# Narrowing all float64 weight pieces in two ScalarE operations through a ring tile, with new costs in the hand-written planner

## The chip, the core and the metric

The kernel runs on one core of one Trainium2 chip. The metric is the device time of one execution in microseconds (us). TensorE multiplies matrices, VectorE and ScalarE work element by element, GpSimd does some elementwise work and indirect transfers, and SyncE issues most of the DMA transfers. Each engine works through its own queue of instructions in the order in which the program wrote them.

## The reference

Three stages follow one another.

```python
# attention: q, k, v are (4, 8, 576, 64) float32
scores = scale * np.matmul(q, k.transpose(0, 1, 3, 2))
kth = np.partition(scores, -32, axis=-1)[..., -32:-31]
attn = softmax(np.where(scores >= kth, scores, -1e9))
x = np.matmul(attn, v)                        # as (2304, 512)

# routing: every token goes to one of 8 experts, 288 tokens each, greedily by logit x @ w_gate
h = np.maximum(x[mask] @ w1[e], 0.0)          # w1: (8, 512, 1024)
x[mask] = h @ w2[e]                           # w2: (8, 1024, 512)

# rational layer
h = x @ w_in                                  # w_in: (512, 2048), float64
g = (a0 + a1*h + a2*h*h + a3*h*h*h) / (1 + |b0|*|h| + |b1|*h*h + 1e-6)
out = (g @ w_out).astype(np.float32)          # w_out: (2048, 512), float64
```

[...] The kernel makes float32 values out of the bits of the float64 ones ("narrowing"), and splits each float32 matrix into a high and a low float16 part, scaled by powers of two, so that TensorE can multiply in float16 with three products.

## The kernel before

`w_in` and `w_out` are cut into 32 pieces of 128 rows by 512 values, 16 of each. A piece is fetched into a raw tile of 128 x 1024 words (`fetch`, L329). Pieces 0 to 5 lie in the tile `win`, 6 to 13 in `wout`, 14 to 17 in `nraw0` to `nraw3` at first; later ones take the places that come free, and the last eight (24 to 31) lie in `region`, which held the first expert's weights.

Narrowing a piece takes ScalarE operations on the top 16 bits of each value (`heads`, L364), then VectorE operations (`mantissa`, L402, with `signed` or `apply_sign`). There are two ways before the change. Pieces 6 to 19 (`quick`, L352) take two ScalarE operations, Abs (L370) and Relu with a scale and a bias (L374), both written into one of three ring tiles; VectorE then ors in the sign bit (`signed`, L392) and the mantissa (`mantissa`, L405). The other 18 pieces take three ScalarE operations in place, Sign into a byte (L380), Abs (L381) and Relu (L382); VectorE then ors in the mantissa (L405) and multiplies by the sign (L409). Behind both, ScalarE squares the piece with a sum (L303); when the four pieces of a block are squared, VectorE works out a power of two as scale, ScalarE writes the high part (`high`, L433) and VectorE the low part (`low`, L437). The low part ends the use of the raw tile, and the next fetch goes into its place.

The order of instructions is worked out when the program is built, by a planner, the class `Flow`. A task has an engine, a cost in us, dependencies and a rank. `Flow` keeps a clock for each engine and always emits the task that can start first, and among equals the one of lowest rank. Costs and start times are the planner's own numbers; on the chip every engine takes its queue in the emitted order. `take` (L159) keeps a task from starting before the task that used the same buffer some turns earlier has been emitted: with `ZR = 3` ring tiles, the first head of a piece waits for the last VectorE part of the piece three before.

The program runs through these stages:

- Attention (up to about 476 us), with an order written out by hand.
- The attention tail, `finish_attention`, a `Flow` of its own called `last`: the last units' softmax, transposes of the weights (`st_transpose`, tile `pt`), their evacuation by ScalarE (`st_spill`, tile `pT`), the product with v (`st_av`, tile `po`), and the router's logits. Tasks of rank 1000 and above fill in: the ScalarE heads of pieces 0 to 5, VectorE's parts of pieces 0 to 2 (`EV = 3`), and `conv_stats` of the first expert's weights. `drain` lets such a task in only where no other task of its engine could start within 0.3 of its cost.
- Routing (511 to about 610 us), seven phases of four iterations in `search`. In each iteration VectorE compares, TensorE counts, VectorE makes the next thresholds. In two gaps of an iteration the planner is called to emit ready tasks of the main `Flow`. The VectorE tasks in a gap have to fit its budget, `J1` or `J3` and `J2`; tasks of ScalarE may run up to `LA` ahead. VectorE's parts of pieces 3 to 31 are put there as halves of 256 values (`in_parts`). `tail` emits one TensorE task, mostly a product of the first expert's weight split, whose result ScalarE copies (L1432).
- `flow.early()` emits what is left until no task is left that is not marked `late`: the blocks of `w_in`, the first three blocks of `w_out`, and the first expert. The fourth block of `w_out` (pieces 28 to 31, rank 6) and the second expert are late. Then `flow.rest()` orders everything else: for each of eight experts 16 units of the rational layer (`add_unit`), weight splits of the next expert (`add_weights`), its products (`add_expert`). Output products need the scales of all blocks of `w_out` (`settle_out`).

```python
def in_parts(cost, fn, deps, rank, late, hv=None):
    w = 512 // (hv or HV)                       # HV = 2
    return [
        flow.add("V", 0.06 + (cost - 0.06) * w / 512, lambda o=o: fn(slice(o, o + w)), deps, rank, late)
        for o in range(0, 512, w)
    ]

def allowed(t, s):                              # in Flow.fill(budget, before)
    v = self.free["V"]
    if t.engine == "V":
        return s <= v + 0.05 and v + t.cost <= v0 + budget + 0.01
    return t.engine != "P" and s <= v + before

J1, J2, J3, T1, T2, T3, J4 = (float(c) for c in "0.6 0.37 0.6 1 1 0 0".split())
```

Of the kernel before, what the change touches and what calls it, by code (L numbers as in the profile page):

```python
# [8 lines left out]
F32 = mybir.dt.float32  # L9
# [175 lines left out]
def kernel(  # L185
# [92 lines left out]
    bias8 = wpool.tile([P, 1], F32, name="bias8")  # L278
    nc.vector.memset(bias8, -896.0 * 2.0**23)
# [50 lines left out]
    SIGN = getattr(mybir.dt, "int8")  # L330
# [17 lines left out]
    QS = int(6)  # L348
    QE = int(20)
    ring, ring_of, ring_users = [], {}, []  # L350

    def quick(n):  # L352
        return QS <= n < QE

    def sign(n):
        return raw_t[n][0].bitcast(SIGN).rearrange("p (n w) -> p n w", w=8)[:, :, 0]

# [6 lines left out]
    def heads(n):  # L364
        top = top_of(n)
        if quick(n):
            def size():
                ring.append(ring.pop(0))
                ring_of[n] = ring[-1]
                nc.scalar.activation(upper_of(n).bitcast(BF16), top.bitcast(BF16), AF.Abs)  # L370

            return [
                ("A", 0.52, size),
                ("A", 0.52, lambda: nc.scalar.activation(  # L374
                    upper_of(n), upper_of(n), AF.Relu, scale=2.0**3, bias=bias16
                )),
            ]
        top = top.bitcast(BF16)
        return [
            ("A", 0.52, lambda: nc.scalar.activation(sign(n), top, AF.Sign)),  # L380
            ("A", 0.52, lambda: nc.scalar.activation(top, top, AF.Abs)),  # L381
            ("A", 0.61, lambda: nc.scalar.activation(  # L382
                value(n).bitcast(U32), top.bitcast(U16), AF.Relu, scale=2.0**19, bias=bias8
            )),
        ]
# [16 lines left out]
    def mantissa(n, o=ALL):  # L402
        mid = raw_t[n][0].rearrange("p (n w) -> p n w", w=2)[:, o, 0]
        up = ring_of[n][:, o] if quick(n) else value(n)[:, o]
        nc.vector.scalar_tensor_tensor(value(n)[:, o], mid, 13, up, op0=OP.logical_shift_right, op1=OP.bitwise_or)  # L405

    def apply_sign(n, o=ALL):
        d = value(n).bitcast(F32)[:, o]
        nc.vector.tensor_tensor(d, d, sign(n)[:, o], op=OP.mult)  # L409
# [4 lines left out]
    EV = 3  # L414

    def add_block(i, n0, dst, s, inv, rows, rank, late, after):
# [54 lines left out]
    with ExitStack() as actx:  # L471
# [61 lines left out]
        with ExitStack() as sctx:  # L533
# [519 lines left out]
            def finish_attention():  # L1053
# [53 lines left out]
                def add_weights_of(u, deps):  # L1107
# [3 lines left out]
                    for hh in range(2):  # L1111
# [15 lines left out]
                        a = last.add("A", 0.67, exp_of, [largest_of[u]] if u in largest_of else [], u)  # L1127
# [5 lines left out]
                def add_turned(u, deps):  # L1133
                    t = last.add("P", 1.1, lambda: st_transpose(u), deps, u)
                    a = last.add("A", 1.01, lambda: st_spill(u), [t], u)
# [88 lines left out]
                for u in range(done["av"], NU):  # L1224
                    if u not in tr_of:
                        tr_of[u] = last.add("A", 1.01, lambda u=u: st_spill(u), [], u)
# [31 lines left out]
                for n in range(6):  # L1258
                    t = []
                    for k in range(3):  # L1260
                        t = [last.add("A", 0.55, lambda n=n, k=k: heads(n)[k][2](), t, 1000 + n)]
                    if n < EV:
                        t = [last.add("V", 0.6, lambda n=n: mantissa(n), t, 1000 + n)]
                        t = [last.add("V", 0.6, lambda n=n: apply_sign(n), t, 1000 + n)]
                for w in (1, 2):
                    for c in range(4):
                        f = last.add("A", 1.04, lambda w=w, c=c: conv_stats(w, 0, c), [], 1000 + (SO if w == 1 else 3) + c)
# [148 lines left out]
        def add_first(which):  # L1416
# [17 lines left out]
            for c in range(4):  # L1434
                t = flow.add("A", 0.95, lambda c=c: conv_hi(which, 0, c), [scaled], -88.0)
# [904 lines left out]
```

## Time and profile before

| | |
|---|---|
| median of three runs | 1280.82 us (1274.78, 1280.82, 1280.97) |
| profiled execution | 1273.43 us, span 1271.7 us |
| TensorE busy in the span | 1142.7 us (90%) |
| VectorE busy | 1152.7 us (91%) |
| ScalarE busy | 1113.9 us (88%) |
| GpSimd busy | 430.7 us (34%) |

The span runs from the first to the last instruction. The profile comes from one execution; its times are us from the start of the span. PE is TensorE's matmul, PEld its weight load, DVE is VectorE, ACT is ScalarE, POOL is GpSimd, SP is SyncE. L303 is line 303 of the kernel. Matmuls overlap, so a busy PE is not PE at its peak. Operations that follow one another on an engine overlap at their ends, so that the distance from start to start is less than the duration.

### The profile page before, as it was taken

Reading aid. Unit: us, or ns where it says so; the run is one execution under the profiler, and the core shown is the slowest. Engines: PE = TensorE matmul, PEld = TensorE weight load, DVE = VectorE, ACT = ScalarE, POOL = GpSimd, SP = SyncE. Lnnn points to the kernel's source line nnn. Section 1 sums busy time; section 2 is a strip of 40 time slices with the busy share of each in tenths; the row PEclk is TensorE's granted clock in tenths of the full one; section 3 lists DMA queues with packets and bytes.
Section 4 is the critical chain, followed back from the end, with each engine's and each line's share of the span. In section 5 each row is a group of like instructions: output and inputs, shape, how many; then the busy total and the mean of one; then the engine's idle time right before and its main releaser. Section 6 shows DMA issues by size and latency. Waiting matters only on the chain.

```text
span 1271.7 us, 26707 instructions
## 1 busy us (share of the span) xinstructions
PE 1142.7 (90%) x9159; PEld 924.6 (73%) x9159; DVE 1152.7 (91%) x4567; ACT 1113.9 (88%) x2150; POOL 430.7 (34%) x431
## 2 busy tenths in 40 slices
PE   6899999999999987687566899999999999999995
PEld 4678787888878876555444677888888888888774
DVE  5999999999999986887789989999999999998895
ACT  5999999999999979867799989998989899887684
POOL 4888888887877850000110001010110001001010
PEclk9999999999999989555688999999999999999998
DMA  5204021020200030921311430303122220200000
GB/s 121 49 10 148 10 57 37 22 49 10 49 1 2 2 133 3 328 105 52 102 55 69 148 129 26 133 26 114 52 86 86 77 76 26 80 1 20 1 20 20
DMA packets 81109, 80.59 MB, mean 63 GB/s; under 512 B 59968, under 2 KB 59968, under 8 KB 80960
## 3 DMA queue, kind: packets, MB, share of 16 engines
q1 hardware_dynamic: 77888, 69.27, 17.1%
q0 software_dynamic: 3072, 9.48, 2.6%
q8 instruction: 76, 1.25, 0.4%
q14 instruction: 73, 0.60, 0.2%
HBM read 69.25 MB, written 9.47 MB: 62 GB/s over the span
## 4 chain that ended last, share of the span: by engine, by line
PE 25%; issue 14%; ACT 6%; DVE 4%; POOL 1%; DMA 1%; POOLq 0%; DVEq 0%
PE pa L1891 3%; PE pa L1893 3%; PE pa L1892 3%; PE ph L1891 3%; PE ph L1892 3%; PE ph L1893 3%; PE po L1892 2%; PE po L1893 2%; PE po L1891 2%; ACT junk L303 1%; POOL out_dram L2261 1%; DMA region<-in_moe_w_dram 1%; DVE wout L437 1%; ACT uv L2152 0%; PE pa L2250 0%
## 5 line engine op out<-in xcount | busy, mean ns | idle before, releaser
L730 DVE MAX8 cd<-sv 128x8 f32<-128x82 f32 (+1 forms) x1008 | 182.5, 229 | 16.5 <-ACT sv L684 16.5
L756 POOL TENSOR_TENSOR win<-sv,sg 128x576 f32<-128x576 f32 x142 | 178.9, 1281 | 52.3 <-ACT sg L751 43.4
L811 POOL TENSOR_TENSOR sv<-ex,sg 128x576 f32<-128x576 f32 x136 | 175.5, 1296 | 44.2 <-DVE sg L808 30.8
L1891 PE MATMUL ph<-x,win 128*128 128x288 f16 x512 | 148.5, 290 | 15.8 <-DVE uv L2173 15.7
L839 PEld LDWEIGHTS po<-vm,pT 128*128 128x128 f32 (+1 forms) x1280 | 143.5, 182 | 19.0 <-ACT pT L823 4.0
L839 PE MATMUL po<-vm,pT 128*128 128x65 f32 (+1 forms) x1280 | 150.2, 266 | 4.8 <-ACT pT L823 3.2
L1892 PE MATMUL po<-g,wout 128*128 128x288 f16 x512 | 146.4, 286 | 4.8 <-DVE g L1882 4.7
L1891 PE MATMUL po<-g,wout 128*128 128x288 f16 x512 | 146.4, 286 | 2.5 <-ACT g L1881 2.5
L1892 PE MATMUL ph<-x,win 128*128 128x288 f16 x512 | 148.5, 290 | 0.0
L1893 PE MATMUL ph<-x,win 128*128 128x288 f16 x512 | 148.4, 290 | 0.0
L1893 PE MATMUL po<-g,wout 128*128 128x288 f16 x512 | 146.4, 286 | 0.0
L1868 POOL DMA_INDIRECT xe<-xrows,rows_i x24 | 24.4, 1017 | 313.6 <-PE pa L1903 160.8
L2261 POOL DMA_INDIRECT out_dram<-ob,tok x24 | 27.3, 1137 | 299.8 <-ACT ob L2257 251.2
L751 ACT ACTIVATE sg<-sv,cut_all 128x576 bf16<-128x576 f32 x142 | 109.2, 779 | 1.4 <-DVE cut_all L736 1.0
L817 PE MATMUL pt<-ident,sv 128*128 128x128 f32 x648 | 93.9, 282 | 13.3 <-POOL sv L811 11.2
L757 DVE MAX8 w<-win 128x8 f32<-128x576 f32 x142 | 105.1, 741 | 0.0
L805 ACT ACTIVATE ex<-sv,nb 128x576 f32<-128x576 f32 x136 | 103.9, 771 | 0.0
L817 PEld LDWEIGHTS pt<-ident,sv 128*128 128x128 f32 x648 | 73.6, 143 | 39.4 <-POOL sv L811 26.7
L671 PE MATMUL s<-region 128*128 128x288 f32 (+5 forms) x400 | 91.7, 385 | 3.7 <-ACT sv L684 2.4
L2149 ACT ACTIVATE z<-ph,inv 128x288 f32<-128x288 f32 x128 | 63.9, 499 | 35.5 <-PE ph L1893 32.5
L684 ACT ACTIVATE sv<-s 128x576 f32<-128x576 f32 x144 | 85.2, 645 | 9.8 <-PE s L671 9.5
L671 PE MATMUL s<-kT,region 128*128 128x288 f32 (+5 forms) x400 | 88.8, 375 | 2.1 <-ACT sv L684 2.0
(361 smaller groups left out, 3510.3 us busy)
## 6 DMA issues: line engine op xcount, KB each, us to landing
region<-in_moe_w_dram SPq DMA_DIRECT2D x16, 2048.0 KB, 8.1
xrows<-x SPq DMA_DIRECT2D x1, 4644.0 KB, 22.6
region<-in_q_dram SPq DMA_DIRECT2D x32, 128.0 KB, 2.9
region<-in_k_dram SPq DMA_DIRECT2D x32, 128.0 KB, 2.9
vm<-in_v_dram SPq DMA_DIRECT2D x32, 128.0 KB, 2.9
wout<-in_moe_w_in_dram SPq DMA_DIRECT2D x8, 511.8 KB, 8.0
region<-in_moe_w_out_dram SPq DMA_DIRECT2D x8, 511.8 KB, 3.5
win<-in_moe_w_in_dram SPq DMA_DIRECT2D x6, 511.8 KB, 6.0
```

The source lines that it names most:

```text
L671: nc.tensor.matmul(ps[p0 : p0 + n, g, o : o + w], qT[:, hh, j, p0 : p0 + n], kT[:, bb, c : c + w], start=True, stop=True,)
L730: nc.vector.max(cd[:, g, :], sv[:, o : o + n])
L751: nc.scalar.activation(sg, sv_t[u, hh], AF.Sign, bias=cut_all[:, 2 * u + hh, 7:8], scale=-OVER, accum_out=t["sum"][:, c : c + 1],)
L756: nc.gpsimd.tensor_tensor(win, sv_t[u, hh], sg, op=OP.mult)
L757: later.append(lambda c=c, win=win: nc.vector.max(t["w8"][:, c, :], win))
L805: nc.scalar.activation(ex, sv, AF.Exp, bias=t["nb"][:, c : c + 1], scale=SCALE)
L811: nc.gpsimd.tensor_tensor(sv, ex, sg, op=OP.mult)
L817: nc.tensor.transpose(pt[:, c // 4, c % 4, :], pr[:, c * P : (c + 1) * P], ident)
L839: nc.tensor.matmul(po[p0 : p0 + n, i, hh, :], sb[:, hh * (R + 1) + c, p0 : p0 + n], vm[:, bb, hh, c, :], start=(c == 0), stop=False,)
L1891: nc.tensor.matmul(acc, ah, bh, start=first, stop=False)
L1892: nc.tensor.matmul(acc, ah, bl, start=False, stop=False)
L1893: nc.tensor.matmul(acc, al, bh, start=False, stop=last)
```

## The change

All 32 pieces take the two ScalarE operations in a ring tile, and VectorE's `signed` and `mantissa`; the form with three operations, with `sign` and `apply_sign`, is gone, and so is its constant `bias8`. In the attention tail pieces 0 to 5 are narrowed whole (`EV = 6`): the ring there consists of three parts of the v tiles that are no longer read, which GpSimd sets to zero. Behind the tail the ring list is emptied and filled with the three ring tiles of before. The costs of many planner tasks are replaced by larger numbers. The budgets of the routing gaps, the ranks, the number of ring tiles and the latencies of the planner stay.

```diff
-    QS = int(6)
-    QE = int(20)
     ring, ring_of, ring_users = [], {}, []
...
     def heads(n):
-        top = top_of(n)
-        if quick(n):
-            def size():
-                ring.append(ring.pop(0))
-                ring_of[n] = ring[-1]
-                nc.scalar.activation(upper_of(n).bitcast(BF16), top.bitcast(BF16), AF.Abs)
...
-        top = top.bitcast(BF16)
+
+        def size():
+            ring.append(ring.pop(0))
+            ring_of[n] = ring[-1]
+            nc.scalar.activation(upper_of(n).bitcast(BF16), top_of(n).bitcast(BF16), AF.Abs)
+
         return [
-            ("A", 0.52, lambda: nc.scalar.activation(sign(n), top, AF.Sign)),
-            ("A", 0.52, lambda: nc.scalar.activation(top, top, AF.Abs)),
-            ("A", 0.61, lambda: nc.scalar.activation(
-                value(n).bitcast(U32), top.bitcast(U16), AF.Relu, scale=2.0**19, bias=bias8
-            )),
+            size,
+            lambda: nc.scalar.activation(upper_of(n), upper_of(n), AF.Relu, scale=2.0**3, bias=bias16),
         ]
...
-    EV = 3
+    EV = 6
...
-            if quick(n):
-                first = flow.add("A", 0.52, lambda n=n: heads(n)[0][2](), t, rank + 0.5, late)
-                t = flow.add("A", 0.52, lambda n=n: heads(n)[1][2](), [first], rank + 0.5, late)
-                t = in_parts(0.6, lambda o, n=n: signed(n, o), [t], rank + 0.4, late)
-                t = in_parts(0.6, lambda o, n=n: mantissa(n, o), t, rank + 0.3, late)
+            if n >= EV:
+                first = flow.add("A", 0.77, lambda n=n: heads(n)[0](), t, rank + 0.5, late)
+                t = [flow.add("A", 0.87, lambda n=n: heads(n)[1](), [first], rank + 0.5, late)]
+                t = in_parts(0.81, lambda o, n=n: signed(n, o), t, rank + 0.4, late)
+                t = in_parts(0.77, lambda o, n=n: mantissa(n, o), t, rank + 0.3, late)
                 take(first, ring_users, ZR, t)
-            else:
-                for k in range(3 if n >= 6 else 0):
-                    t = [flow.add("A", (0.52, 0.52, 0.61)[k], lambda n=n, k=k: heads(n)[k][2](), t, rank + 0.5, late)]
-                if n >= EV:
-                    t = in_parts(0.6, lambda o, n=n: mantissa(n, o), t, rank + 0.4, late)
-                    t = in_parts(0.6, lambda o, n=n: apply_sign(n, o), t, rank + 0.3, late)
             norms.append(
-                flow.add("A", 0.61, lambda n=n, g=g: square(value(n).bitcast(F32), sq[:, g : g + 1]), t, rank + 0.2, late)
+                flow.add("A", 0.86, lambda n=n, g=g: square(value(n).bitcast(F32), sq[:, g : g + 1]), t, rank + 0.2, late)
             )
...
-            t = flow.add("A", 0.61, lambda g=g: high(g), [scaled] + (lasts[-1] if lasts else []), rank + LOWS, late)
-            t = flow.add("V", 0.66, lambda g=g: low(g), [t], rank + LOWS + 0.1, late)
+            t = flow.add("A", 0.75, lambda g=g: high(g), [scaled] + (lasts[-1] if lasts else []), rank + LOWS, late)
+            t = flow.add("V", 0.74, lambda g=g: low(g), [t], rank + LOWS + 0.1, late)
...
-                for n in range(6):
-                    t = []
-                    for k in range(3):
-                        t = [last.add("A", 0.55, lambda n=n, k=k: heads(n)[k][2](), t, 1000 + n)]
-                    if n < EV:
-                        t = [last.add("V", 0.6, lambda n=n: mantissa(n), t, 1000 + n)]
-                        t = [last.add("V", 0.6, lambda n=n: apply_sign(n), t, 1000 + n)]
+                for i in (2, 2, 0):
+                    free = v_pad[i][0].rearrange("p b h r d -> p (b h r d)").bitcast(U32)
+                    ring.append(free[:, 512 * len(ring) % 1024 :][:, 0:512])
+                    nc.gpsimd.memset(ring[-1], 0)
+                for n in range(EV):
+                    first = last.add("A", 0.77, lambda n=n: heads(n)[0](), [], 1000 + n)
+                    t = [last.add("A", 0.87, lambda n=n: heads(n)[1](), [first], 1000 + n)]
+                    t = [last.add("V", 0.6, lambda n=n: signed(n, ALL), t, 1000 + n)]
+                    t = [last.add("V", 0.6, lambda n=n: mantissa(n), t, 1000 + n)]
+                    take(first, ring_users, ZR, t)
...
+        ring.clear()
+        ring_users.clear()
         for i in range(ZR):
```

The other costs that change: in the tail `exp_of` from 0.67 to 0.77, `st_spill` from 1.01 to 1.16, `conv_stats` from 1.04 to 1.26. For the first expert's weights `conv_hi` from 0.95 to 1.13 and the copy of a product from 0.27 to 0.38, and the squares of x from 0.52 to 0.82. In `add_weights` `conv_stats` from 1.04 to 1.26, `conv_hi` from 0.95 to 1.16, `conv_lo` from 0.63 to 0.75. In `add_unit` the six ScalarE tasks from 0.43, 0.5, 0.5, 0.46, 0.38, 0.46 to 0.49, 0.59, 0.63, 0.54, 0.44, 0.53, and the seven VectorE tasks from 0.43 to 0.48 to 0.45 to 0.51; its TensorE tasks stay at 1.47.

## Rows read from the trace of the kernel before

**Rows 1.** Stretches: length, busy us (count) of PE, PEld, DVE, ACT, POOL; PEclk, DMA.
```profile
476.00:507.00 31.00, 25.95 (x205) 20.32 (x203) 20.17 (x72) 29.95 (x39) 0.96 (x1) 1.00 0.01 2
...
511.00:596.70 85.70, 71.45 (x793) 49.41 (x794) 74.35 (x360) 64.97 (x124) 6.20 (x14) 0.50 0.49 174
596.70:614.00 17.30, 6.55 (x80) 5.36 (x78) 7.73 (x29) 14.10 (x15) 1.94 (x4) 0.50 0.12 35
614.00:671.20 57.20, 35.35 (x248) 26.53 (x248) 53.36 (x150) 50.50 (x96) 9.21 (x9) 0.80 0.27 87
671.20:690.00 18.80, 11.49 (x65) 7.63 (x65) 18.09 (x64) 17.91 (x39) 0.00 (x0) 0.73 0.31 113
690.00:760.00 70.00, 62.65 (x510) 49.41 (x508) 62.18 (x153) 63.80 (x125) 0.84 (x1) 1.00 0.34 121
760.00:1200.00 440.00, 439.14 (x3619) 354.13 (x3618) 408.99 (x1081) 387.54 (x812) 36.90 (x52) 1.00 0.18 59
1200.00:1272.00 72.00, 55.13 (x432) 42.13 (x430) 55.92 (x141) 49.16 (x107) 6.28 (x11) 0.95 0.06 18
```

**Rows 2.** Timeline of ScalarE in the attention tail: start, length, line, output, input.
```profile
485.96 1.21 ACT L823 ACTIVATE pT<-pt 128x1152 f32<-128x1152 f32 x1
...
491.00 1.41 ACT L380 ACTIVATE win<-win 128x512 int8<-128x512 bf16 x1
492.16 1.21 ACT L823 ACTIVATE pT<-pt 128x1152 f32<-128x1152 f32 x1
```

**Rows 3.** Waits, 470 to 507 us: in total, times, longest.
```profile
PE po L839 <- ACT pT L823: 3.2, 4, 1.3
```

**Rows 4.** Waits in the routing stretch, 511 to 597 us.
```profile
DVE over L1561 <- PE pl L1497: 6.0, 18, 0.6
...
PE pl L1428 <- ACT w2s L1432: 0.9, 1, 0.9
```

**Rows 5.** Line L380, the first of three operations: min/median/max ns, first and last start.
```profile
L380 ACT ACTIVATE region<-region x8: 1322/1329/1388, 561.2 to 607.9; 128x512 int8<-128x512 bf16 x8
L380 ACT ACTIVATE win<-win x6: 1322/1373/1416, 476.8 to 499.8; 128x512 int8<-128x512 bf16 x6
L380 ACT ACTIVATE wout<-wout x4: 1354/1398/1462, 637.6 to 652.7; 128x512 int8<-128x512 bf16 x4
```

**Rows 6.** Line L370, the first of two operations, 611.7 to 700 us.
```profile
L370 ACT ACTIVATE ring<-wout x2: 779/786/792, 634.3 to 635.9; 128x512 bf16<-128x512 bf16 x2
L370 ACT ACTIVATE ring<-nraw x1: 771/771/771, 616.1 to 616.1; 128x512 bf16<-128x512 bf16 x1
```

**Rows 7.** Timeline of ScalarE in routing, two-operation pieces.
```profile
529.72 0.77 ACT L370 ACTIVATE ring<-wout 128x512 bf16<-128x512 bf16 x1
530.35 0.36 ACT L1432 ACTIVATE w1s<-pl 128x256 f16<-128x256 f32 x1
530.60 0.87 ACT L374 ACTIVATE ring<-ring,bias 128x512 uint16<-128x512 uint16 x1
531.32 1.38 ACT L370 ACTIVATE ring<-wout 128x512 bf16<-128x512 bf16 x2
...
532.82 0.65 ACT L303 ACTIVATE junk<-win 128x512 bf16<-128x512 f32 x1
...
533.45 1.58 ACT L374 ACTIVATE ring<-ring,bias 128x512 uint16<-128x512 uint16 x2
```

**Rows 8.** Timeline of ScalarE after routing, a three-operation piece.
```profile
637.56 1.35 ACT L380 ACTIVATE wout<-wout 128x512 int8<-128x512 bf16 x1
638.64 0.51 ACT L1877 ACTIVATE hT<-pe 128x288 f16<-128x288 f32 x1
```

**Rows 9.** Groups of VectorE, 511 to 611.7 us: busy us, mean ns; idle before.
```profile
L392 DVE SCALAR_TENSOR_TENSOR ring<-wout,ring 128x256 uint16<-128x256 uint16 x16 | 7.0, 438 | 0.0
L405 DVE SCALAR_TENSOR_TENSOR wout<-wout,ring 128x256 uint32<-128x256 uint32 x16 | 6.6, 414 | 0.0
...
L409 DVE TENSOR_TENSOR win<-win 128x256 f32<-128x256 f32 x6 | 2.5, 415 | 0.0
```

More of the change, by code (lines that the diff above doesn't have):

```diff
@@ L329 @@
     arrived = [Mark() for _ in range(NP)]
-    SIGN = getattr(mybir.dt, "int8")
     def fetch(slot, n=None):
@@ L1134, in add_turned @@
                     t = last.add("P", 1.1, lambda: st_transpose(u), deps, u)
-                    a = last.add("A", 1.01, lambda: st_spill(u), [t], u)
+                    a = last.add("A", 1.16, lambda: st_spill(u), [t], u)
                     hold(t, "pt", 1, [a])
@@ L1225, in finish_attention @@
                     if u not in tr_of:
-                        tr_of[u] = last.add("A", 1.01, lambda u=u: st_spill(u), [], u)
+                        tr_of[u] = last.add("A", 1.16, lambda u=u: st_spill(u), [], u)
                 for u in range(done["av"], NU):
@@ L1434, in add_first @@
             for c in range(4):
-                t = flow.add("A", 0.95, lambda c=c: conv_hi(which, 0, c), [scaled], -88.0)
+                t = flow.add("A", 1.13, lambda c=c: conv_hi(which, 0, c), [scaled], -88.0)
                 for o in range(c * 1024, (c + 1) * 1024, 256):
                     p = flow.add("P", 0.6, lambda o=o: product(o), [t, copies[0]], -88.0)
-                    copies.append(flow.add("A", 0.27, lambda o=o: copy(o), [p], -90.0))
+                    copies.append(flow.add("A", 0.38, lambda o=o: copy(o), [p], -90.0))
                     take(p, pl_users, 2, [copies[-1]])
@@ L1444 @@
         norms = [
-            flow.add("A", 0.52, lambda t=t: square(x[:, t, 0:DM], xs[:, t : t + 1]), (), XSR) for t in late_tiles
+            flow.add("A", 0.82, lambda t=t: square(x[:, t, 0:DM], xs[:, t : t + 1]), (), XSR) for t in late_tiles
         ]
@@ L2003, in add_weights @@
             got = flow.add("D", 5.8, lambda: load_w(which, e), reading("raw", which, e - 1), rank(0))
-        sums = [flow.add("A", 1.04, lambda c=c: conv_stats(which, e, c), [got], rank(c)) for c in range(4)]
+        sums = [flow.add("A", 1.26, lambda c=c: conv_stats(which, e, c), [got], rank(c)) for c in range(4)]
         steps = scale_steps(which, e)
@@ L2009, in add_weights @@
         for c in range(4):
-            t = flow.add("A", 0.95, lambda c=c: conv_hi(which, e, c), [scaled] + hs[-1:], rank(5 + c))
+            t = flow.add("A", 1.16, lambda c=c: conv_hi(which, e, c), [scaled] + hs[-1:], rank(5 + c))
             if c == 0:
@@ L2014, in add_weights @@
         for c in range(8):
-            all_.append(flow.add("V", 0.63, lambda c=c: conv_lo(which, e, c), [hs[c // 2]], rank(5 + c // 2) + 0.1))
+            all_.append(flow.add("V", 0.75, lambda c=c: conv_lo(which, e, c), [hs[c // 2]], rank(5 + c // 2) + 0.1))
         split_of[which, e] = hs + all_
@@ L2196, in add_unit @@
         p = flow.add("P", 1.47, into, x2_of[e] + last["into"], u)
-        a1 = flow.add("A", 0.43, size, [p, scales[e]], u)
-        a3 = flow.add("A", 0.5, cube, [p, scales[e]], u)
-        v1 = flow.add("A", 0.5, below, [a1], u + 0.05)
-        g1 = flow.add("V", 0.43, below2, [v1], u + 0.05)
-        g2 = flow.add("V", 0.44, cube2, [a1, a3], u + 0.1)
-        v3 = flow.add("V", 0.48, cube3, [g2], u + 0.1)
-        a4 = flow.add("A", 0.46, log, [g1], u + 1.0)
-        a5 = flow.add("A", 0.38, exp, [a4], u + 1.0)
-        v2 = flow.add("V", 0.43, near, [a5], u + 1.2)
-        v4 = flow.add("V", 0.43, nearer, [v2], u + 1.2)
-        v5 = flow.add("V", 0.48, ratio, [v3, v4], u + 1.2)
-        a6 = flow.add("A", 0.46, halves, [v5, bounds[e]], u + 2.0)
-        v6 = flow.add("V", 0.48, lambda: st["steps"][1](), [a6], u + 2.1)
+        a1 = flow.add("A", 0.49, size, [p, scales[e]], u)
+        a3 = flow.add("A", 0.59, cube, [p, scales[e]], u)
+        v1 = flow.add("A", 0.63, below, [a1], u + 0.05)
+        g1 = flow.add("V", 0.45, below2, [v1], u + 0.05)
+        g2 = flow.add("V", 0.45, cube2, [a1, a3], u + 0.1)
+        v3 = flow.add("V", 0.51, cube3, [g2], u + 0.1)
+        a4 = flow.add("A", 0.54, log, [g1], u + 1.0)
+        a5 = flow.add("A", 0.44, exp, [a4], u + 1.0)
+        v2 = flow.add("V", 0.45, near, [a5], u + 1.2)
+        v4 = flow.add("V", 0.45, nearer, [v2], u + 1.2)
+        v5 = flow.add("V", 0.51, ratio, [v3, v4], u + 1.2)
+        a6 = flow.add("A", 0.53, halves, [v5, bounds[e]], u + 2.0)
+        v6 = flow.add("V", 0.51, lambda: st["steps"][1](), [a6], u + 2.1)
         p2 = flow.add("P", 1.47, out_of, [v6] + last["out"] + w_out_done[f // 4], u + OUT)
```

25 lines of the change are left out of this document (6 added, 19 removed).

## The prediction

> **What bounds the kernel now.** I read the stages first [rows 1]: in each row compare the length with the busy time of TensorE, VectorE and ScalarE. From 760 to 1200 us TensorE is busy 439.14 of 440 us, so there it alone sets the pace and nothing that the other engines save counts. The stretches before it are different. From 614 to 671.2 us VectorE is busy 53.36 and ScalarE 50.50 of 57.2 us, TensorE only 35.35; from 671.2 to 690 us both are again over 95% busy, and up to 760 us they stay near 90% while TensorE loses 7.35 us. TensorE's queue after routing is a fixed amount of work, so every microsecond by which ScalarE and VectorE are later in getting the weights narrowed between 614 and 760 us moves the end by about a microsecond. The routing stretch before, 511 to 596.7 us, is a fixed loop of handshakes between VectorE and TensorE; ScalarE is busy 64.97 of 85.7 us there, and 14.10 of the next 17.3 us. What is done there is free; what is left over is paid for after 614 us.
>
> Then I read the narrowing itself. A three-operation piece stands in two places: eight of 18 ran between 561 and 610 us, inside routing and its end, four after it, six in the attention tail [rows 5]. Of the two-operation pieces only three had their heads (the ScalarE operations) after routing [rows 6]. Of the VectorE halves, 16 + 16 + 6 and, in two rows not shown, 6 + 1 ran in the routing gaps: 45 [rows 9]. The code has 116 halves in the flow (pieces 3 to 31, four each), so 71 came after.
>
> **The change, part by part.**
>
> *Price of a head.* What counts on a full engine is the distance from start to start, not the duration. A two-operation piece: 529.72 to 530.35 is 0.63, 530.60 to 531.32 is 0.72, together 1.35 us [rows 7]. A three-operation piece: 637.56 to 638.64 is 1.08 [rows 8]; I take that for the first two operations, which last about the same, and 0.72 for the third: 2.88 us. One piece saves 1.53 us of ScalarE; 18 pieces save 27.5. A square takes 532.82 to 533.45, 0.63 us [rows 7].
>
> The rule of the Trainium skill speaks against so large a saving: its page "ScalarE: Activation LUTs", section "What ACT_TABLE_LOAD costs", has one element per cycle for every function, 186 ns + 0.833 ns for each element with immediate operands, less 93 ns of overlap. That would be 0.52 us for each of the two operations where the row has 1.08, so 1.76 us for a three-operation piece. The trace decides and I use 2.88; by the page the sum below would come out 4 x 1.12 = 4.5 us later.
>
> *Attention tail.* Six pieces lose 1.53 us each: 9.2 us of ScalarE in a stretch where it is busy 29.95 of 31 us. But the end of the stretch is set by TensorE and VectorE, with the units' products and the last tiles' logits. What ScalarE contributes there is late evacuation of pT: it is queued behind long operations, as at 485.96 and 492.16 us, right behind the operation that starts at 491.00 and lasts 1.41 [rows 2]. TensorE waited 3.2 us for pT [rows 3]. The planner had counted these operations at 0.55, so it put too many ahead of a pT; with true costs most of that goes. Against this VectorE gets three more whole pieces, 12 x 0.42 = 5 us, in a stretch where it is busy 20.17 of 31: hidden, or up to 1 us of it on the chain. The three memsets on GpSimd, busy 0.96 of 31 us, cost nothing. I take -2.5 us; bounds 0 (the waits stay) and -9.2 (ScalarE alone paces the tail).
>
> *Routing loop.* VectorE's work goes into gaps that the planner fills by cost: one of 0.6 and one of 0.37 in each of 28 iterations. A half cost 0.06 + 0.54/2 = 0.33 and fitted both. Now a half costs 0.06 + 0.75/2 = 0.435 or 0.06 + 0.71/2 = 0.415: it fits the gap of 0.6 once and the gap of 0.37 never, though the operation itself is unchanged (0.41 to 0.44 us [rows 9]). The loop is not faster for the empty gap: VectorE waits for TensorE 18 times there even with the halves in [rows 4]. The one gain is the 0.9 us that TensorE stood waiting for ScalarE's copy of w2s [rows 4] behind long heads: -1 us (bound 0).
>
> *How much narrowing is left over.* Heads began at 529.72 [rows 7]; squares of pieces 3 to 5 now come ahead, 3 x 0.63 = 1.9 us, so first halves near 533.5 us. A phase of four iterations is 85.7 us / 7 = 12.2 us; up to 596.7 us there are 63/12.2 x 4, about 20 gaps of 0.6, so about 20 halves, five pieces. And now every piece from 6 on needs one of three ring tiles, freed only by its last half. So heads run three pieces ahead of VectorE at most: eight pieces (6 to 13), while before 11 two-operation and eight three-operation heads ran in or right behind routing. Most of ScalarE's 14.10 us from 596.7 to 614 stay unused.
>
> *After routing, ScalarE.* Heads before: 3 x 1.35 + 4 x 2.88 = 15.6 us. Now 18 x 1.35 = 24.3: +8.7. Squares: 14 pieces were squared in routing, now about 11: +3 x 0.63 = 1.9. Together +10.6 us. VectorE: 84 halves left (26 pieces x 4 - 20) instead of 71: 13 x 0.42 = +5.5 us. The idle time that could take it up, 614 to 690 us [rows 1]: ScalarE 57.2 - 50.50 + 18.8 - 17.91 = 7.6, VectorE 4.5 us. Part of that idle time is waiting for gathers and first products, so I let half of it, 3.8, take up work: 10.6 - 3.8 = 6.8. Then the last block of w_out: its four pieces lay narrowed by ScalarE before 614 us (rows of the tile region, last start 607.9 [rows 5]); now they come last in rank, behind the first units, and 4 x 1.35 of heads, 16 halves and the settling of the scales stand in a row before the first output product can start. I put 4 us on this (bounds 0 and 4 x (1.35 + 0.63) = 7.9). Stage sum +10.8; bounds +1 (VectorE's 5.5 less its 4.5 of idle time, ScalarE hidden) and 10.6 + 7.9 = +18.5 (nothing taken up).
>
> *Costs of the expert stage.* No work changes, only the order. Costs are now durations, above spacing (0.77 against 0.63 [rows 7]); the planner sees ScalarE fuller than it is. TensorE is at 439.14 of 440 us already, so little is to be won: 7.35 us of loss up to 760 and the last 72 us, where TensorE is busy 55.13. I take 0; bounds -7 and +7 (1.5% of 440).
>
> Sum: -2.5 - 1 + 10.8 + 0 = +7.3 us. Against the profiled execution, span 1271.7 and time 1273.4, that gives 1280.7. The median of the three runs is 1280.82, 7.4 above the profiled time, and the lowest of them 1274.78. I carry half of that difference, 3.7: 1284.4, said as 1284. From here on times are on that scale, where no change is 1277.1.
>
> **The rivals.**
>
> *The tail pays for it (faster).* Place: 476 to 507 us. If ScalarE, 97% busy, really paces the tail, all 9.2 us come off; with -1 in routing and a loss after it of only 3 us (all 7.6 us of idle time taken up, 10.6 - 7.6) the sum is -7.2: 1270. It decides for faster once the tail gives 5.4 us more than the stage after routing costs. For it: 29.95 of 31. Against: TensorE waited only 3.2 us for pT [rows 3].
>
> *It cancels (same).* The idle time takes up the surplus and the last block's pieces slip in among the early ones: -2.5 - 1 + 3 to 5, so 1277 to 1279. For it: ScalarE and VectorE idle 12 us together after routing. Against: the ring couples the two engines, so one's wait becomes the other's.
>
> *The new order stalls TensorE (slower still).* Costs above spacing make the planner hold ScalarE full, and TensorE finds an operand late in a stage where it now waits for nothing: +7 on top, 1291. For it: duration and spacing differ by a fifth [rows 7]. Against: overstated costs err on the side of operands that are ready early.
>
> **How the numbers follow.** About 0.5%, 6.4 us, is what a measurement of this kernel can tell from no change. Forecast 0.35, new order on top of it 0.10, cancelling 0.33, tail 0.22. So slower 0.45, same 0.33, faster 0.22; the likeliest single case is the forecast, +7.3, with its own range 1280 to 1291. The whole range reaches from a little under the tail's 1270 to a little over the new order's 1291: 1268 to 1295, which leaves out large gains and the sum of both losses.
>
> **What would show it.** In the profile after: no operation of 1.33 us left on ScalarE; the tail some 2 to 3 us shorter, with pT evacuated right behind its transposes. In routing, VectorE halves near 20 instead of 45, one to an iteration, and phases of about 12.1 us. ScalarE nearly empty between 598 and 611 us, where it was full. After routing, about 18 pieces' heads, ScalarE without gaps to 690 us and beyond, the first unit's product and the first output product some 7 to 11 us later counted from the end of routing. Then TensorE saturated up to the end. I am wrong if two halves still go into an iteration, if heads run more than three pieces ahead, if the stage after routing is no longer than before, or if the tail gives more than 5 us.

## The result, and the profile after

The changed kernel takes 1293.87 us (median of 4 runs, 1293.50 to 1294.21), the kernel before 1280.49 us (4 runs): a ratio of 1.0113, 95% interval 1.0092 to 1.0135. It is slower by more than the forecast of 1284: outside the forecast's own range of 1280 to 1291, inside the whole range of 1268 to 1295. The profiled execution took 1293.90 us with a span of 1291.8. That is 20.1 us more than the span of before, but the execution profiled before was the fastest of its kernel; between the medians lie 13.4 us.

First the stages of the changed kernel, in the same columns and, up to 1200 us, the same stretches as [rows 1]:

```profile
476.00:507.00 31.00, 27.17 (x215) 21.27 (x213) 24.75 (x80) 22.97 (x38) 2.52 (x2) 1.00 0.01 2
...
511.00:596.70 85.70, 73.47 (x834) 51.54 (x835) 66.53 (x330) 45.30 (x95) 6.48 (x15) 0.50 0.49 176
596.70:614.00 17.30, 4.68 (x41) 3.52 (x39) 9.54 (x35) 2.95 (x7) 4.03 (x2) 0.50 0.09 28
614.00:671.20 57.20, 36.27 (x242) 26.85 (x243) 48.16 (x136) 50.85 (x102) 8.11 (x8) 0.74 0.26 83
671.20:690.00 18.80, 8.11 (x38) 4.87 (x37) 15.49 (x42) 17.09 (x36) 0.00 (x0) 0.68 0.33 114
690.00:760.00 70.00, 52.83 (x386) 39.74 (x385) 58.20 (x162) 61.30 (x121) 0.00 (x0) 0.87 0.19 68
...
760.00:1200.00 440.00, 435.10 (x3583) 350.51 (x3581) 404.84 (x1070) 385.00 (x806) 36.05 (x52) 1.00 0.20 67
```

ScalarE lost 7 us of work in the tail, 20 in routing and 11 between 596.7 and 614 us, where it now has almost nothing to do. TensorE is busy 9.8 us less than before between 690 and 760 us, and its granted clock there is 0.87 where it was 1.00. From 760 to 1200 us it loses 4.9 of 440 us, where it lost 0.9 before.

The tail and routing can be timed by GpSimd: the memset of the ring tiles begins right behind the tail, the first gather of expert rows right behind routing. The kernel before, then the changed one (timeline of GpSimd):

```profile
510.88 1.45 POOL L1304 MEMSET ring<- 128x512 uint32 x3 [33.92 <-PEq L1272]
...
613.47 1.15 POOL L1868 DMA_INDIRECT xe<-xrows,rows_i  x1 [13.74 <-PEq L1841]
```

```profile
509.65 1.58 POOL L1279 MEMSET ring<- 128x512 uint32 x3 [29.92 <-DVEq L1245]
...
609.66 1.15 POOL L1843 DMA_INDIRECT xe<-xrows,rows_i  x1 [13.66 <-DVEq L1816]
611.12 4.00 POOL L1843 DMA_INDIRECT xe<-xrows,rows_i  x1 [0.31 <-issue]
615.42 0.92 POOL L1843 DMA_INDIRECT xe<-xrows,rows_i  x1 [0.30 <-issue]
```

So in these two profiles the tail ends 1.2 us earlier, and routing is 2.6 us shorter. The end of the tail scatters, though: in the profiles of the experiments below it lies at 514.87 us where the tail is the old one (the control of the rank), and between 507.85 and 512.31 where it has the new form. The size of its gain is not settled. Now the other end of the stage: the first in-product and the first output product of TensorE, in the kernel before and in the changed one (tile views: min/median/max ns, first and last start):

```profile
L1891 PE MATMUL ph<-x,win x512: 282/286/448, 661.5 to 1249.9; 128*128 128x288 f16 x171
...
L1891 PE MATMUL po<-g,wout x512: 282/286/288, 689.9 to 1258.5; 128*128 128x288 f16 x171
```

```profile
L1866 PE MATMUL ph<-x,win x512: 282/286/448, 665.6 to 1269.0; 128*128 128x288 f16 x171
...
L1866 PE MATMUL po<-g,wout x512: 282/286/444, 714.4 to 1278.6; 128*128 128x288 f16 x171
```

From the first gather to the first output product it was 689.9 - 613.47 = 76.4 us; now it is 714.4 - 609.66 = 104.7. From there to the end of the span it was 581.8 us and is 577.4, and by then TensorE had got products of the next expert done (24, from 708.3 us), of which there were none before the first output product in the kernel before. The account of the spans: -3.8 + 28.3 - 4.4 = +20.1 us.

Three of TensorE's waits between 614 and 760 us grew, before and after: for VectorE's copy of the next expert's transposed tokens (`xT`), for a step in settling the scales (`ev_m`), and for the gathers.

```profile
PE pa L1903 <- DVE xT L1882: 10.6, 1, 10.6
...
PE pa L1318 <- DVE ev_m L1325: 2.4, 1, 2.4
...
PE pe L1903 <- DMA xe<-xrows,rows_i: 1.4, 2, 0.8
```

```profile
PE pa L1878 <- DVE xT L1857: 15.8, 1, 15.8
...
PE pa L1293 <- DVE ev_m L1300: 9.7, 1, 9.7
PE pe L1878 <- DMA xe<-xrows,rows_i: 4.6, 2, 3.7
```

The 3.2 us more for the gathers come mostly from one slow gather (last section); it was no part of the forecast.

Why the first output product is late is seen by following the last piece of `w_out` (timelines of ScalarE, VectorE and TensorE put together):

```profile
675.96 1.37 ACT L358 ACTIVATE ring<-region 128x512 bf16<-128x512 bf16 x2
677.19 0.48 ACT L2124 ACTIVATE z<-ph,inv 128x288 f32<-128x288 f32 x1
...
687.07 1.04 ACT L301 ACTIVATE junk<-region 128x1024 bf16<-128x1024 f32 x1
...
697.33 0.85 ACT L362 ACTIVATE ring<-ring,bias 128x512 uint16<-128x512 uint16 x1
...
701.97 0.64 ACT L301 ACTIVATE junk<-region 128x512 bf16<-128x512 f32 x1
...
705.42 0.16 DVE L1300 TENSOR_REDUCE ev_m<-s_out 128x1 f32<-128x16 f32 x1
...
713.40 0.28 DVE L2057 TENSOR_SCALAR sgr<-r_out,bt,inv 128x16 f32<-128x16 f32 x1
...
714.35 0.28 PE L1866 MATMUL po<-g,wout 128*128 128x288 f16 x1 [1.09 <-issue]
```

The last piece's first head is the second of the two at 675.96, its second head starts at 697.33. Between them lie 20 us in which ScalarE works mostly on the first units (lines 2124 to 2142, the first of them at 677.19), whose ranks are lower, and on the statistics of the next expert's weights (687.07). Then come the halves, the square (701.97), the settling of the scales (705.42) and the units' factors (713.40). The 9.7 us for `ev_m` are TensorE's wait for this block.

The forecast's counts in routing came out. VectorE's halves between 507 and 609 us:

```profile
L370 DVE SCALAR_TENSOR_TENSOR ring<-wout,ring x10: 439/442/451, 538.2 to 588.5; 128x256 uint16<-128x256 uint16 x10
...
L382 DVE SCALAR_TENSOR_TENSOR wout<-wout,ring x9: 416/419/421, 542.7 to 590.7; 128x256 uint32<-128x256 uint32 x9
```

19 halves instead of 45. And ScalarE's timeline from the last copy in routing to the next operation shows the idle 16 us; the next operation in its queue is a square, which waits for VectorE's last half of that piece:

```profile
594.62 0.38 ACT L1407 ACTIVATE w2s<-pl 128x256 f16<-128x256 f32 x1 [0.68 <-PE pl L1404]
611.02 0.67 ACT L301 ACTIVATE junk<-wout 128x512 bf16<-128x512 f32 x1 [16.02 <-DVE wout L382]
```

### The profile page after: what moved, and what is told of

The parts are those of the page before. It is cut to its first block, busy times and chain, and to the rows that moved or that the text cites. A ratio compares the mean times of both kernels' runs of the same rounds, so it can differ in the third digit from the quotient of the medians.

```text
span 1291.8 us, 26689 instructions
## 1 busy us (share of the span) xinstructions
PE 1153.2 (89%) x9159; PEld 931.4 (72%) x9159; DVE 1152.1 (89%) x4560; ACT 1084.4 (84%) x2132; POOL 433.0 (34%) x434
## 4 chain that ended last, share of the span: by engine, by line
PE 26%; issue 14%; DVE 6%; ACT 4%; DMA 2%; POOL 1%; POOLq 0%; DVEq 0%
PE pa L1866 3%; PE pa L1868 3%; PE pa L1867 3%; PE ph L1866 3%; PE ph L1868 3%; PE ph L1867 3%; PE po L1866 3%; PE po L1867 3%; PE po L1868 3%; DMA region<-in_moe_w_dram 1%; ACT junk L301 1%; POOL out_dram L2236 1%; DVE wout L412 1%; DVE w1s L1344 1%; ACT ring L358 1%
## 5 line engine op out<-in xcount | busy, mean ns | idle before, releaser
L699 DVE MAX8 cd<-sv 128x8 f32<-128x82 f32 (+1 forms) x1008 | 182.1, 228 | 17.7 <-ACT sv L653 17.7
L1843 POOL DMA_INDIRECT xe<-xrows,rows_i x24 | 27.6, 1148 | 327.3 <-PE pa L1878 163.0
L2236 POOL DMA_INDIRECT out_dram<-ob,tok x24 | 24.7, 1028 | 309.4 <-ACT ob L2232 256.8
L786 PE MATMUL pt<-ident,sv 128*128 128x128 f32 x648 | 94.3, 284 | 11.3 <-POOL sv L780 9.6
L792 ACT ACTIVATE pT<-pt 128x1152 f32<-128x1152 f32 x72 | 82.0, 1139 | 10.0 <-PE pt L786 10.0
```

The costliest lines, as they stand in the source:

```text
L699: nc.vector.max(cd[:, g, :], sv[:, o : o + n])
L786: nc.tensor.transpose(pt[:, c // 4, c % 4, :], pr[:, c * P : (c + 1) * P], ident)
```

## The experiments

The runs of one group shared a chip with runs of the kernel before, whose median there is the base of the ratio: 1279.43 in the first group, 1279.15 in the second, 1278.14 in the third, 1279.53 in the last.

### First group: which part carries the loss

**The second gap at 0.45.**

```diff
-J1, J2, J3, T1, T2, T3, J4 = (float(c) for c in "0.6 0.37 0.6 1 1 0 0".split())
+J1, J2, J3, T1, T2, T3, J4 = (float(c) for c in "0.6 0.45 0.6 1 1 0 0".split())
```

> The changed kernel with one number different: the second gap of a routing iteration takes 0.45 instead of 0.37, so that a half of 0.435 or 0.415 fits it. Theory of the gaps (halves that no longer fit routing are paid for behind it): VectorE runs about 40 halves in routing instead of 19, five more pieces have their heads and squares there, about 10 us of ScalarE and 9 us of VectorE leave the stage behind routing, and the time falls from 1294 to about 1284. Rival, the late last block: the last piece of w_out waits for its rank behind the first units, not for the engines; then the halves move but the first output product stays within 5 us of 714 us, and the time is 1290 or more.

1282.42 us, ratio 1.0030 (1.0018 to 1.0041): 11.4 us less than the changed kernel, from one number. 35 halves run in routing (16 + 2 and 16 + 1, between 507 and 609 us), and eight pieces that lie in `wout` have their squares there, where four had. The time is what the theory of the gaps expected, and below the rival's 1290. The first output product moves to 703.9 us, more than the 5 us that the rival allowed, but it is still late: the last piece's halves end at 674.7, but its square starts at 686.17, again behind units and weight statistics.

**The last block ahead of the units.**

```diff
-RL = [float(v) for v in "-2 1 3 6".split()]
+RL = [float(v) for v in "-2 1 3 -2".split()]
```

> The changed kernel with the rank of the fourth block of w_out (pieces 28 to 31) at -2 instead of 6, so that its narrowing comes ahead of the first units. Theory of the late last block: in the changed kernel the second ScalarE operation of the last piece starts at 697.3 us, behind unit work, and the first output product at 714.4 us, against 689.9 in the kernel before; with the rank ahead the first output product comes at 690 to 697 us and the time is 1275 to 1282. Rival, the amount of work: ScalarE and VectorE have too much to do between 614 and 710 us; then the units are later by as much as the block is earlier, and the time is 1288 to 1294.

1282.00 us, ratio 1.0029 (1.0014 to 1.0044), 11.9 us less than the changed kernel with not one operation moved into routing. First output product:

```profile
L1866 PE MATMUL po<-g,wout x512: 282/286/297, 700.5 to 1265.7; 128*128 128x288 f16 x171
```

It is 14 us earlier, 3.5 short of what was expected; the in-product stays at 664.2. The time lies at the top of what the theory of the late last block expected, and outside that of the rival. TensorE's wait of 9.7 us for `ev_m` is gone.

**Two operations everywhere, old costs.** All numbers in the planner as before; the narrowing as in the changed kernel.

```diff
-t = in_parts(0.81, lambda o, n=n: signed(n, o), t, rank + 0.4, late)
-t = in_parts(0.77, lambda o, n=n: mantissa(n, o), t, rank + 0.3, late)
+t = in_parts(0.6, lambda o, n=n: signed(n, o), t, rank + 0.4, late)
+t = in_parts(0.6, lambda o, n=n: mantissa(n, o), t, rank + 0.3, late)
...
```

> The changed kernel (all pieces in two ScalarE operations through the ring) with all planner costs as in the kernel before. Theory of the gaps: a half costs 0.33 again, fits both gaps, some 40 to 45 halves run in routing, and the time is 1275 to 1281, so the new costs carry the whole loss. Rival, the ring: with three ring tiles for all pieces the heads can't run ahead whatever the costs, pieces 28 to 31 are late all the same, and the time is 1287 or more.

1284.15 us, ratio 1.0048 (1.0033 to 1.0064): between the two. 39 halves run in routing, so the gaps are filled; but the first output product comes at 702.0 us, and ScalarE is busy 1.61 us between 596.7 and 614. With the old costs the narrowing costs about 5 us.

**The old costs in the expert stage only.**

```diff
-a1 = flow.add("A", 0.49, size, [p, scales[e]], u)
+a1 = flow.add("A", 0.43, size, [p, scales[e]], u)
...
```

> The changed kernel with only the costs of the expert stage as before (the sixteen units' tasks and the weight splits of experts 1 to 7). Theory of the gaps and that of the late last block: the loss lies before these costs matter, 1291 to 1296. Rival, the new order of the expert stage stalls TensorE: 1284 to 1288, with less idle time of TensorE from 760 us on.

1293.86 us, ratio 1.0125 (1.0107 to 1.0143): the time of the changed kernel. As the cause of the loss the rival is out. It had expected less idle time of TensorE from 760 us on, and there is more: 430.72 us busy of the 440 up to 1200, where the changed kernel has 435.10.

### Second group: tail, both edits, ring, control

**The tail's part alone.** The kernel before with the tail of the change.

```diff
-    QS = int(6)
+    QS = int(0)
...
-    EV = 3
+    EV = 6
...
-                for n in range(6):
-                    t = []
-                    for k in range(3):
-                        t = [last.add("A", 0.55, lambda n=n, k=k: heads(n)[k][2](), t, 1000 + n)]
...
+                for n in range(EV):
+                    first = last.add("A", 0.77, lambda n=n: heads(n)[0][2](), [], 1000 + n)
...
```

> The kernel before with only the attention tail of the change: pieces 0 to 5 in two ScalarE operations with the ring in the v tiles, whole pieces 0 to 5 in VectorE there, and the tail's new costs; pieces 20 to 31 keep the three operations in place, and all costs behind the tail are as before. Theory (the heads in place are free, because ScalarE has nothing else to do from 597 to 611 us): the tail's gain of 1.2 us and some of routing's 2.6 us stay and nothing is paid behind routing, 1275 to 1279 where the kernel before runs at 1279.4. Rival (fewer ScalarE operations are better wherever they stand, only the gaps were mis-set): no better than the kernel with the second gap at 0.45, 1282.

1275.99 us, ratio 0.9980 (0.9964 to 0.9997). The pieces that stay in place use ScalarE's time behind routing, as in [rows 1]:

```profile
596.70:614.00 17.30, 7.99 (x101) 6.34 (x100) 9.32 (x38) 14.24 (x16) 1.41 (x3) 0.50 0.10 33
```

The first output product comes at 691.7 us. It is a hair faster than before, less than 0.5%. The time is as expected, the reason is not seen: in its profile the tail ends at 512.31 us and routing takes 103.6 us, where the kernel before has 510.88 and 102.6.

**Second gap and rank together.** The two diffs of the first group.

> The changed kernel with both edits, the second gap at 0.45 and the rank of the fourth block of w_out at -2. If the two losses are separate (work left over, and the block that is behind the units): their gains of about 11.5 and 12 us add up in part, first output product at 690 to 695 us, 1274 to 1278. If they are one loss seen from two sides: 1280 to 1283, as each alone.

1276.17 us, ratio 0.9981 (0.9965 to 0.9997), and

```profile
L1866 PE MATMUL po<-g,wout x512: 282/286/447, 689.9 to 1258.9; 128*128 128x288 f16 x171
```

17.7 us less than the changed kernel, where the two alone gave 11.4 and 11.9: they add up in part. Given the one, the other is worth 6 us.

**Four ring tiles.**

```diff
-    ZR = 3
+    ZM = 4
...
-        get["junk"] = lambda: lpool.tile([P, 1024], BF16, name="junk", bufs=1)
+        get["junk"] = lambda: lpool.tile([P, 1024], getattr(mybir.dt, "int8"), name="junk", bufs=1)
```

> The changed kernel with the second gap at 0.45 and four ring tiles instead of three; to make room, the squares' unused output is int8 instead of bf16. Theory of the ring (heads can't run further ahead than the ring has tiles): one more piece has its head in ScalarE's idle time from 594 to 611 us, 1.4 us of ScalarE leaves the stage behind, and heads that waited inside routing come earlier; 1278 to 1281, and ScalarE is busy more than 4.5 us between 596.7 and 614 (3.3 with three tiles). Rival, the ring doesn't bind: 1282 to 1283 and the same busy time there.

1283.87 us, ratio 1.0042 (1.0023 to 1.0060): no gain over three tiles, though the edit also changes the type of the squares' output, and ScalarE busy 3.77 us between 596.7 and 614, not 4.5. Yet the first output product is at 689.4 us, 14.5 earlier than with three tiles. TensorE gives 4.2 us of it back later, in a stretch where three tiles lost 1.5; the stretch 760 to 1200 us with three, then with four tiles:

```profile
760.00:1200.00 440.00, 438.49 (x3616) 353.64 (x3614) 402.17 (x1072) 387.13 (x812) 35.86 (x52) 1.00 0.19 64
```

```profile
760.00:1200.00 440.00, 434.32 (x3554) 348.75 (x3552) 403.98 (x1063) 383.23 (x800) 33.00 (x48) 0.99 0.17 58
```

**Control: the rank in the kernel before.** The diff of `RL`, there.

> The kernel before with the rank of the fourth block of w_out at -2 instead of 6, the control for that edit. Theory of the late last block: there its pieces have their heads before 611 us, so the rank costs it little; the first output product moves by less than 5 us and the time stays within 3 us of 1279.4. Rival (the rank is simply wrong in both kernels): it gains as in the changed kernel, 8 us or more, 1268 to 1272.

1278.54 us, ratio 0.9998 (0.9982 to 1.0015): no change in the time, as expected. The first output product came 9 us later (699.0), where less than 5 was expected; 4.0 of the 9 lie ahead of the first gather, which came at 617.47. In this kernel, where the block's heads have run by the end of routing, the rank gains nothing.

### Third group: heads in ScalarE's idle time

**Pieces 28 to 31 in place.** Three operations, as before the change, for four pieces of the changed kernel.

```diff
+            if n >= 28:
+                for k, c in enumerate((1.36, 1.36, 0.79)):
+                    t = [flow.add("A", c, lambda n=n, k=k: in_place(n)[k](), t, rank + 0.5, late)]
+                t = in_parts(0.77, lambda o, n=n: mantissa(n, o), t, rank + 0.4, late)
+                t = in_parts(0.77, lambda o, n=n: apply_sign(n, o), t, rank + 0.3, late)
```

> The changed kernel with one part undone: pieces 28 to 31 keep the three ScalarE operations in place, which need no ring tile, with their durations as costs (1.36, 1.36, 0.79) and two VectorE operations of 0.77; gaps and ranks as in the changed kernel. Theory (the ring keeps the last block's heads out of ScalarE's idle time from 594.6 to 611 us): the heads of three pieces or more run before 611 us, though they take twice as long; the first output product comes at 690 to 703 us instead of 714 and the time is 1280 to 1285. Rival (the block is late by its rank alone, not by its heads): its VectorE halves are behind the units all the same, first output product at 709 us or later, 1289 or more.

1282.57 us, ratio 1.0034 (1.0012 to 1.0057), first output product at 695.8. The longer heads run in the idle time; the first of the three operations there, and the stretch:

```profile
L364 ACT ACTIVATE region<-region x4: 1328/1387/1392, 596.5 to 604.6; 128x512 int8<-128x512 bf16 x4
```

```profile
596.70:614.00 17.30, 4.95 (x58) 3.98 (x57) 8.65 (x32) 10.79 (x13) 2.79 (x3) 0.50 0.14 45
```

Four pieces with twice the ScalarE work make the kernel 11.3 us faster, and that work stands where ScalarE was idle in the changed kernel (10.79 us busy there instead of 2.95). That the place is the reason fits, but the two runs that follow limit it.

**The same with the second gap at 0.45, and with the rank besides.**

> Pieces 28 to 31 in three operations in place, and the second gap at 0.45. If the work left over behind routing and the late last block are two losses, this gives what the second gap and the rank gave together, 1273 to 1278. If the 16 us of idle time are already of no use once the gaps take their halves: 1280 to 1284, as the second gap alone.

> All three edits: pieces 28 to 31 in three operations in place, the second gap at 0.45, the fourth block of w_out at rank -2. If heads in ScalarE's idle time are free, the 4 x 1.35 = 5.4 us of heads that the same kernel without the first edit pays behind routing go: 1270 to 1274 where that kernel ran at 1276.2. If they only swap one order for another: 1275 to 1279.

1278.69 us, ratio 1.0007 (0.9993 to 1.0022), and 1281.03 us, ratio 1.0022 (1.0004 to 1.0040). The first is just above what was expected for two losses. The second is a miss: all three edits are slower than two, by 5 us against gap and rank. Their first output products come at 689.3 and 693.1 us, and TensorE is busy 433.66 and 434.76 of 440 us from 760 to 1200, as with four ring tiles. So the heads in the idle time are worth 11.3 us in the changed kernel, 3.7 once the second gap is right, and with the rank besides they cost 4.9. Which tasks turn the gain round was not followed.

### Last: the new costs without the new narrowing

> The narrowing of the kernel before (pieces 6 to 19 through the ring, the other 18 in three operations in place, three whole pieces in VectorE in the tail) with the new costs everywhere, 1.36, 1.36 and 0.79 for the three operations and 0.77 for a whole multiplication by the sign. If the halves that no longer fit the second gap cost by themselves: about 20 halves in routing, the surplus is paid for behind it, 1284 to 1289. If they cost only together with the ring (the in-place heads of the last blocks still run in ScalarE's idle time, so the first output product is not late): within 3 us of the kernel before.

1293.49 us, ratio 1.0113 (1.0089 to 1.0138): both expectations are far too low. The costs alone make the whole loss, 14 us against the kernel before. 24 halves run in routing (four groups of 6 in lines 392, 405 and 409). The last block's heads do run early, from 597.28 us; what is left over costs at another place. TensorE's longest wait from 614 us on, and its first in-product, 30 us later than before:

```profile
PE pa L1318 <- DVE xT L1882: 32.7, 1, 32.7
```

```profile
L1891 PE MATMUL ph<-x,win x512: 282/286/447, 691.6 to 1268.6; 128*128 128x288 f16 x171
```

During that wait VectorE works mostly on left-over narrowing, halves (L405, L409) and low parts (L437), most of it of `w_out`, and only then copies `xT`; the scales of `w_out` are ready (`r_out`) ahead of the first in-product (timeline of VectorE):

```profile
668.18 0.76 DVE L409 TENSOR_TENSOR wout<-wout 128x256 f32<-128x256 f32 x2
...
670.20 0.51 DVE L1882 SCALAR_TENSOR_TENSOR xT<-pa,s_x,xT 128x288 f16<-128x288 f32 x1
...
687.83 0.22 DVE L1387 TENSOR_SCALAR r_out<-i_out,settle 128x16 f32<-128x16 f32 x1
```

So here it is not the last block that holds the units up, but the narrowing that routing did not take, ahead of them in VectorE's queue. The second gap at 0.45 was not tried with this narrowing, and the costs of halves, squares, high and low parts and of the first expert's weights were raised together: which of them carries the 14 us is not shown.

## Why the prediction came out as it did

The direction was right, and so was the first half of the mechanism: the new costs empty the second gap, and the narrowing left over is paid for behind routing. The size was not right: +7.3 us by the sum, +13.4 between the medians. The whole range holds the result only because its upper end was put over 1291, the time of the rival with the new order of the expert stage. That rival did not happen, so this part is luck.

- *Attention tail*, -2.5: it ends 1.2 us earlier, within a scatter of some 4 us. TensorE's waits for pT are gone, as forecast, but the tail now ends with the narrowing in VectorE (the mantissa of piece 5 starts at 505.7 us).
- *Routing*, -1: it gave 2.6 us. From the second on, phases are 12.0 us (from one start of `asel` on GpSimd to that of the next phase), where one of before took 13.1.
- *Halves in routing*, about 20: 19. **Shown as a cause in the changed kernel**: fitting the gap to the new cost takes off 11.4 us with nothing else changed. The new costs make the whole loss with the old narrowing too, at 24 halves.
- *The ring*: a fourth tile brought nothing, so its share as a throttle inside routing was not shown. Heads that need no ring tile do run in ScalarE's idle 16 us, and four such pieces take off 11.3 us, but 3.7 with the second gap right, and nothing with the rank right besides. With old costs the two-operation form everywhere loses about 5 us, with new ones none beyond what the costs lose already (1293.87 against 1293.49).
- *After routing, ScalarE* +8.7 of heads: 19 second heads from 612 us on, where 18 were counted. This count held, but the price did not come the way that it was put, as time of a full ScalarE: from 614 to 690 us ScalarE's busy time fell by 0.5 us and VectorE's by 7.8 [rows 1], while TensorE's waits grew. The half of ScalarE's idle 7.6 us that was to take up work was not taken up.
- *First products*, both 7 to 11 us later counted from the end of routing: the first in-product is (665.6 - 609.66 against 661.5 - 613.47, 7.9 us), the first output product is 28.3 later.
- *The last block of w_out*, 4 us, bounds 0 and 7.9: **this is the term that failed.** The prediction saw that its pieces lie behind the first units, but priced only their own work. Their price is the queue that they wait behind: 20 us between two heads of one piece, the first output product 24.5 us later than before. Setting only the rank right takes off 11.9 us, and 6.3 where the second gap is right already.
- *Costs of the expert stage*, 0: right, 1293.86 with the old ones.
- *TensorE saturated up to the end*: not quite, it loses 4.9 us from 760 to 1200 us. The expert stage's costs are not the reason, since with the old ones it loses 9.3.

The last block's term can't be added to that of the halves: both edits together give 17.7 us, more than the loss. And the run with the new costs alone loses as much without a late last block. What the two have in common is narrowing that routing did not take. By itself it need not cost much: with the rank right and the halves still left over, the kernel is 2.6 us above the kernel before. Which task stands behind the left-over work in a queue, and who waits for it, decides the price. As a rule for both losses this is argued from the two traces, not tested.

Of the rivals, a tail that pays is out by the time alone, nothing cancels, and the new order of the expert stage is not what costs. An operation in place had been priced by its row. By the page "ScalarE: Activation LUTs" of the Trainium skill, section "What ACT_TABLE_LOAD costs", its 512 elements would last, as an estimate, 186 + 0.833 x 512 ns, 0.61 us. The trace does not agree: the four in the run with pieces 28 to 31 in place took 1.33 to 1.39.

Two things stay open. With three edits that each shorten the changed kernel by 11 to 12 us, the sums do not add: two together gave 17.7 and 15.2, all three 12.8. And an early first output product is no guarantee: among the kernels that have it between 689 and 696 us the medians run from 1276.0 to 1283.9, and in some of them TensorE loses up to 6.3 us between 760 and 1200. Which tasks make up that loss was not followed.

## What to carry to other kernels

A planner's costs and the budgets that they are held against are one set of numbers: costs raised to what the trace shows, with budgets left as they were, emptied a gap that could still be filled at next to no cost (phases took 12.0 us with 35 halves in routing as with 19). The raised costs alone lost 1.1%, and refitting one budget won back most of what the changed kernel had lost. In the changed kernel a task that slipped behind others cost the queue that it then stood in, not its own length, so when work is left over, ask first which of it is the last to be let in and who needs it. And shorter is not always better: twice the ScalarE work in a stretch of idle time beat half of it in a busy one, by 11.3 us. But such gains are tied to the order around them: with gap and rank set right the same edit lost 4.9.

## What the runs showed of the hardware

TensorE's clock after a wait. In the changed kernel it stood still for 15.85 us before 665.04 us and for 7.40 before 679.29. Its products then followed one another at twice the usual distance, 0.24 us, until about 671 us the first time, and the second time until the next wait, which begins behind the product at 684.77 us; at 691.77 us they stood 0.12 apart (timeline of TensorE):

```profile
665.58 0.45 PE L1866 MATMUL ph<-x,win 128*128 128x288 f16 x1
665.82 0.45 PE L1867 MATMUL ph<-x,win 128*128 128x288 f16 x1
...
679.29 0.40 PE L1866 MATMUL ph<-x,win 128*128 128x288 f16 x1 [7.40 <-DVE uv L2148]
...
691.77 0.29 PE L1866 MATMUL ph<-x,win 128*128 128x288 f16 x1
691.89 0.29 PE L1867 MATMUL ph<-x,win 128*128 128x288 f16 x1
```

The granted clock of 660 to 690 us was 0.61 (0.75 before), of 690 to 720 us 0.75 (1.00 before), mixtures of its two levels, 1.2 GHz (0.5) and 2.4 GHz (1.0). So products right behind these waits took twice the time. What that adds over the whole span is not settled: TensorE's busy time rose from 1142.7 to 1153.2 us, but it is 1146.3 in the kernel with the wait of 32.7 us.

One gather: the second one behind routing took 4.00 us on GpSimd where its neighbours took 1.15 and 0.92, and TensorE waited 3.7 us for it. The longest of the first nine gathers lay between 3.8 and 5.2 us in eleven of the fourteen profiles, at 1.5 in the kernel before. What it depends on was not tried.
